# Another start offset for the stationary operands of a seven-product matrix multiply

## The chip, the cores and the metric

The kernel runs on one core of a Trainium2 chip. The metric is the device time of one execution in microseconds, taken as the median of several runs. Beside the runs there is one profiled execution, which gives the engines' busy times and a trace of every instruction and DMA.

## The reference

Linear attention without a softmax, an RMS norm with a gain, and a two-layer GELU network, all in float32:

```python
kv = np.einsum('bhsd,bhse->bhde', k, v)
out = np.einsum('bhsd,bhde->bhse', q, kv)
rms = np.sqrt(np.mean(out * out, axis=-1, keepdims=True) + 1e-06)
attn = out / rms * g_norm                      # (8, 8, 576, 64)
x = attn.transpose(0, 2, 1, 3).reshape(4608, 512)
h = x @ w_in                                   # (4608, 512) @ (512, 2048)
g = 0.5 * h * (1.0 + erf(h / sqrt(2)))
return g @ w_out                               # (4608, 2048) @ (2048, 512)
```

## The kernel before

**Chunks.** The 4,608 tokens are taken in nine chunks `c` of 512. For every chunk the kernel computes the attention output, transposed so that the 512 features lie on the partitions, the first layer `x @ w_in` with GELU, and the second layer. While chunk `c` is in its two layers, the attention of chunk `c + 1` and the key-value sums of chunk `c + 2` are done in between: small matmuls of L183 (`sum_kv`), L236 (`project_pair`) and L288 (`fold`). The order of all this is written out by hand, and every load and store goes out on SyncE's queue (SPq in the profile).

**Two halves of a number.** TensorE is fed in the float32r form. To keep float32 precision each operand is split into a high and a low part, and each product is made of three: high by high, low by high, high by low.

**Seven products.** Chunks 0 and 1 (`PLAIN = 2`) multiply in the ordinary way (L687, L714: 512 moving columns). From chunk 2 on the first layer, and from chunk 3 on (`FAST = 3`) the second layer too, cut both operands in 2 x 2 blocks and take seven products of sums of blocks instead of eight (Strassen's scheme in Winograd's form). The sums of the weights' blocks are formed once, in chunk 1 and 2, and sent to DRAM as `products`; those of `x` and `g` are formed for each chunk.

**The first layer** has 8 steps `j` of seven products. `product(at, j, k, ...)` (L545) issues one of them: two blocks of 128 rows times three parts, so six matmuls, at L552. The stationary operand is a 128 x 128 piece of a weight, the moving one 256 columns of `x`. In chunk 2 the seven products of a step come together (`layer1_pair`, L559). From chunk 3 on they are issued in two parts, products 0 to 3 (`first_part`) and 4 to 6 (`second_part`); the second part of step j stands behind the first part of step j + 1, and the small matmuls of the next chunks stand behind some of the second parts.

**The second layer** of chunks 3 to 8 has 28 ticks (`TICKS`, L464) of twelve matmuls (L1230). Here the activations are stationary and the weights are moving, 256 columns of them.

**Where the weights come from.** They do not all fit. A key, ("in", j, i) or ("out", k, n), names 512 KB: two products of the first layer or one tick of the second. Thirteen keys (`RESIDENT`) stay in SBUF. All others are loaded again for every chunk, in the order of use, into a ring of six tiles: `fetch(n)` (L498) takes tile `RING[n % 6]`, and `used` (L522) requests the key six places on when a key has been used up. So a load has some five keys' time to land.

**Where operands start.** All these tiles lie in one pool, one after the other, each a multiple of 256 bytes long, so that their starts agree modulo 256; the pieces that one matmul takes lie at multiples of 512 bytes within a tile. The tiles of the ring and of the resident keys are 64 elements, 256 bytes, longer than their 1,024 elements. `AWAY`, 48 elements or 192 bytes, says how far into such a tile the weights are put; the tiles of `x` and of the activations are always used from their start. `aligned(c, key)` (L508) names the loads that are put at 0 instead:

- of the first layer, keys with i = 0 (products 0 and 1): all eight steps in chunk 2; steps 0, 2, 3, 4 and 5 in chunks 3, 4 and 5; steps 0, 2, 3 and 4 in chunks 6 and 7; step 0 in chunk 8;
- of the second layer, the first tick, (0, 0).

From a moving operand's start to that of its stationary one it is then, modulo 256 bytes, 192 in the first layer (0 for aligned keys) and 64 in the second, where the weights are the moving side (0 in the first tick).

**How the trace shows it.** In the timeline a group x12 of L552 is two products, and a group x6 one. `h<-x,w_in` names the PSUM bank and the two operands by their tiles; since tiles are used again for other things, `w_in`, `w_out`, `x`, `s` and `r` there are names of places and no longer of contents.

Of the kernel before, what the change touches and what calls it, by code (L numbers as in the profile page):

```python
# [9 lines left out]
F32R = mybir.dt.float32r  # L10
# [13 lines left out]
FAST = 3  # L24
# [13 lines left out]
def linear_attn_rms_gelu_ffn(  # L38
# [18 lines left out]
    NT, DM = out.shape  # L57
    B, NP = kv_main.shape[:2]
# [5 lines left out]
    NCH = NT // CH  # L64
# [25 lines left out]


    LINE = 16
    AWAY = 3 * LINE
    KEPT_IN = [f"w_out{i}" for i in (4, 5, 6, 7)]
    KEPT_OUT = [f"w_out{i}" for i in (8, 9, 10, 11)] + [f"w_in{i}" for i in (13, 14, 15)]
    KEPT_OUT += ["r0", "w_in4"]
# [7 lines left out]
    def block_tile(name, dtype):  # L104
        return const.tile([P, 2 * DM + EXTRA.get(name, 0)], dtype, name=name)
# [64 lines left out]
    def rows(r):  # L170
        return slice(r * D, (r + 1) * D)
# [211 lines left out]
    def reused(i, dtype=F32):  # L383

        if i not in kept:
            kept[i] = block_tile(f"w_in{i}", dtype)
        return kept[i][:, :2 * DM]
# [10 lines left out]
    def product_out(at, src, eng=nc.sync):  # L398

        key, n = at[:-1], at[-1]  # L400
        if key in RESIDENT and key[0] == "out":
            if key not in resident:
                t = block_tile(KEPT_OUT[KEPT_KEYS.index(key[1:])], F32R)
                resident[key] = t[:, AWAY:AWAY + 2 * DM]
            to = resident[key][:, n * DM:(n + 1) * DM].rearrange("p (a n) -> p a n", a=2)
            eng.dma_start(out=to.bitcast(F32), in_=src.bitcast(F32))
            return
        if key not in products:
            products[key] = dram.tile([P, 2 * DM], F32, name="_".join(map(str, ("products", *key))))
        to = products[key][:, n * DM:(n + 1) * DM]  # L410
        eng.dma_start(out=to.rearrange("p (a n) -> p a n", a=2), in_=src.bitcast(F32))  # L411
# [3 lines left out]
    def combine(j, second):  # L415

        if not second:
            whole.clear()
            for a in range(2):
                w = parts["in", 2 * j + a].bitcast(F32)  # L420
                whole[a] = work.tile([P, DM], I32, name="z", bufs=2).bitcast(F32)
                nc.vector.tensor_tensor(out=whole[a], in0=w[:, HI], in1=w[:, LO], op=ALU.add)
                t = parts["in", 2 * j + a].rearrange("p (a n) -> p a n", a=2)
                if a == 0:
                    product_out(place_in(j, 0), t[:, :, :HALF])
                    product_out(place_in(j, 4), t[:, :, HALF:])
                else:
                    product_out(place_in(j, 3), t[:, :, HALF:])
        a11, a12 = whole[0][:, :HALF], whole[0][:, HALF:]
        a21, a22 = whole[1][:, :HALF], whole[1][:, HALF:]  # L430
        s = work.tile([P, DM], I32, name="w", bufs=2).bitcast(F32)
        s = s.rearrange("p (a n) -> p a n", a=2)
        if second:
            adds = ((s[:, 0], a11, ALU.subtract, a21), (s[:, 1], a12, ALU.subtract, whole[2]))
        else:
            whole[2] = s[:, 1]
            adds = ((s[:, 0], a21, ALU.add, a22), (s[:, 1], s[:, 0], ALU.subtract, a11))
        for o, x, op, y in adds:
            nc.vector.tensor_tensor(out=o, in0=x, in1=y, op=op)
        stage[j, second] = s  # L440
# [23 lines left out]
    TICKS = [(0, 0), (0, 1), (0, 2), (2, 0), (2, 1), (0, 3), (2, 2), (2, 3)]  # L464
# [19 lines left out]
    resident = {}  # L484
    queue = []
# [12 lines left out]
    def fetch(n):  # L498

        if n < len(queue):  # L500
            key = queue[n][1]
            i = RING[n % len(RING)]
            reused(i, F32R)
            away = 0 if aligned(*queue[n]) else AWAY
            ring[n] = kept[i][:, away:away + 2 * DM]
            nc.sync.dma_start(out=ring[n].bitcast(F32), in_=products[key])

    def aligned(c, key):  # L508

        kind, j, k = key  # L510
        if kind == "out":
            return (j, k) == TICKS[0]
        if k:
            return False
        n = 8 if c < FAST else 6 if c + 2 < B else 5 if c + 1 < NCH else 1
        return j < n and (c < FAST or j != 1)

    def operand(c, key):
        at = c, key
# [2 lines left out]
    def used(c, key):  # L522
        if (c, key) in place:
            n = place[c, key]
            ring.pop(n)
            fetch(n + len(RING))
# [5 lines left out]
        return name, block_tile(name, dtype)[:, :2 * DM]  # L532

    def keep(key):
        t = resident[key] = block_tile(KEPT_IN[key[1]], F32R)[:, AWAY:AWAY + 2 * DM]
        nc.sync.dma_start(out=t.bitcast(F32), in_=products[key])

    SETS = (("h0", "h1"), ("acc0", "acc1"), ("acc2", "acc3"))
# [266 lines left out]
    for d in range(0, 2 * D, BLK):  # L805
        h = d // D * D
        nc.gpsimd.tensor_tensor(
            out=fold[:, d:d + BLK], in0=ident[:, h:h + BLK], in1=ident[:, h + BLK:h + 2 * BLK],
# [27 lines left out]
    def sum_squares(n):  # L836
# [12 lines left out]
        out=half_g, in0=ps[:, :1], scalar1=0.5, scalar2=None, op0=ALU.mult  # L849
# [3 lines left out]
        out=sums[:, :P], lhsT=ones, rhs=eps, start=True, stop=False,  # L853
# [4 lines left out]
        out=root_g, in0=half_g, scalar1=D ** 0.5, scalar2=None, op0=ALU.mult  # L858
# [9 lines left out]
    for half in range(2):  # L868
# [6 lines left out]
        out=sums[:, :n_fold].rearrange("p (g b) -> p g b", g=2), lhsT=fold,  # L875
# [3 lines left out]
    for half in range(2):  # L879
        nc.scalar.activation(  # L880
            out=first.block((1, half)),
# [10 lines left out]
    for half in range(2):  # L892
# [3 lines left out]
            out=first.o_all[:, half], in0=first.ps.pop((0, half)), scalar=root_g, in1=bc,  # L896
            op0=ALU.mult, op1=ALU.mult,
        )
        n = 2 + half
        bc = bank(f"acc{n}")  # L900
        for t in range(NG):
            for h in range(2):
                at = column(n, t) + h
                nc.tensor.matmul(
                    out=bc[rows(h), t * P:(t + 1) * P],
# [150 lines left out]
    def later(c, i):  # L1056

        if 2 <= i < NJ2:
            raw_out(i - 2)
        if i == 7:  # L1060
            sums[c] = attn[c + 1].fold()
        if i in (5, 7):
            load_kv(c + 2, (i - 5) // 2)
        if i == 9:
            attn[c + 2].load(0)
        if i == 15:
            place_kv(c + 2, range(NP))
            attn[c + 2].load(1)
        send()
        if i == 13:  # L1070
            for n in range(2):
                fetch(n)
        if i == 15:
            for n in range(2, len(RING)):
                fetch(n)
# [39 lines left out]
    for s in range(PLAIN * NF):  # L1115
        c, i = divmod(s, NF)
# [31 lines left out]
        else:  # L1148
            spread_matmuls(c, i)
            g[s] = gelu(h.pop(s))  # L1150
            nxt, k = attn[c + 1], SQUARES.index(i) if i in SQUARES else None
# [10 lines left out]
            elif i - 1 in EARLY:  # L1162
                n = EARLY.index(i - 1)
# [209 lines left out]
    for c in range(PLAIN, FAST):  # L1373
        for j in range(NJ2):
# [28 lines left out]
            if j > 3:  # L1403
                keep(RESIDENT[j - 4])
# [92 lines left out]
```

## Time and profile before

| what | value |
|---|---|
| median of three runs | 789.97 us (789.1 to 792.87) |
| span of the profiled execution | 790.6 us |
| TensorE matmuls, busy | 779.8 us, 99% of the span, 6,460 instructions |
| TensorE weight loads, busy | 727.1 us, 92% |
| VectorE, busy | 569.6 us, 72% |
| ScalarE, busy | 351.7 us, 44% |
| DMA, mean rate over the span | 302 GB/s |

TensorE has two rows in a profile, PE for matmuls and PEld for the loads of stationary operands, which overlap the matmuls. Matmuls are pipelined: one of 256 columns is shown as some 276 ns long, but the next one starts some 113 ns after it. What one costs in a full stream is therefore the distance between starts, not the duration. The timeline merges equal instructions that follow each other: start of the first, time from there to the end of the last, and their count.

### The profile page before, as it was taken

The page shows a single profiled execution, that of the slowest core. Times are in us where ns is not written, and L with a number is a line of the kernel's source. Part 1 is how long each engine was busy: PE and PEld are TensorE (multiplying, and loading weights), DVE is VectorE, ACT ScalarE, POOL GpSimd, SP SyncE. Part 2 cuts the span into 40 slices and gives each one's busy share as a digit, 9 for nine tenths or more (in the row PEclk, how much of TensorE's full clock was granted, in tenths as well). Part 3 has the DMA queues.
Part 4 walks back from the last instruction along what each step waited for, and adds up shares of the span by engine and source line. Part 5 has one row for each costly group of instructions (what it writes and reads, how often), then busy time and mean ns, then how long its engine had stood idle before and what let it go on. Part 6 is the DMA issues. An engine that isn't in the chain of part 4 may idle for free.

```text
span 790.6 us, 16438 instructions
## 1 busy us (share of the span) xinstructions
PE 779.8 (99%) x6460; PEld 727.1 (92%) x6460; DVE 569.6 (72%) x1035; ACT 351.7 (44%) x667; POOL 162.6 (21%) x142
## 2 busy tenths in 40 slices
PE   8999999999899999999999999999999999999998
PEld 6888878888789998999999999999999999999998
DVE  3998866898467673779377956786589658965683
ACT  3777535433262232447053624363436343632461
POOL 1000040421150302350027001800161016101200
PEclk9999999999999999999999999999999999999999
DMA  9991307999999579998989799969997989799974
GB/s 347 406 390 55 121 9 272 355 349 370 344 358 320 196 278 374 364 400 293 374 333 358 259 368 333 384 231 320 322 360 252 313 307 323 248 327 343 329 252 163
DMA packets 88800, 239.10 MB, mean 302 GB/s; under 512 B 8852, under 2 KB 30612, under 8 KB 88724
## 3 DMA queue, kind: packets, MB, share of 16 engines
q1 hardware_dynamic: 88720, 238.06, 84.0%
q8 instruction: 51, 0.84, 0.4%
q14 instruction: 25, 0.20, 0.1%
q10 hardware_dynamic: 4, 0.00, 0.0%
HBM read 199.23 MB, written 34.08 MB: 295 GB/s over the span
## 4 chain that ended last, share of the span: by engine, by line
PE 94%; DMA 3%; DVE 1%; SPq 1%; issue 0%; ACT 0%; DVEq 0%; ACTq 0%
PE acc L1230 21%; PE acc L552 19%; PE acc L714 16%; PE h L552 16%; PE h L687 10%; PE a L1230 8%; PE a L236 2%; PE a L183 2%; DMA kv_main<-kv_main 1%; DMA w_in<-products_in 1%; DMA w_in<-qT 1%; PE h L677 0%; DVE x L346 0%; DVE w_out L655 0%; SPq L411 0%
## 5 line engine op out<-in xcount | busy, mean ns | idle before, releaser
L714 PE MATMUL acc<-w_out,gh 128*128 128x512 f32 x312 | 97.1, 392 | 0.0
L687 PE MATMUL h<-x,w_in 128*128 128x512 f32 x360 | 87.4, 391 | 0.6 <-DVE x L346 0.6
L687 PEld LDWEIGHTS h<-x,w_in 128*128 128x128 f32 x360 | 67.3, 188 | 15.6 <-DVE x L346 1.3
L714 PEld LDWEIGHTS acc<-w_out,gh 128*128 128x128 f32 x312 | 57.7, 188 | 12.3 <-issue 0.4
L700 ACT ACTIVATE gh<-h 128x512 fp32r<-128x512 f32 x39 | 23.3, 598 | 93.1 <-PE h L687 62.8
L714 PE MATMUL acc<-w_out,gl 128*128 128x512 f32 x156 | 60.7, 389 | 0.0
L552 PE MATMUL h<-w_in,w_in 128*128 128x256 f32 x420 | 54.8, 281 | 3.3 <-DMA w_in<-products_in 3.3
L1230 PE MATMUL acc<-w_in,w_out 128*128 128x256 f32 x444 | 55.3, 277 | 0.0
L552 PEld LDWEIGHTS h<-w_in,w_in 128*128 128x128 f32 x420 | 51.5, 192 | 3.9 <-issue 3.9
L1230 PEld LDWEIGHTS acc<-w_in,w_out 128*128 128x128 f32 x444 | 52.8, 188 | 0.0
L552 PE MATMUL acc<-w_out,w_in 128*128 128x256 f32 x390 | 52.2, 280 | 0.0
L552 PEld LDWEIGHTS acc<-w_out,w_in 128*128 128x128 f32 x390 | 47.7, 188 | 1.2 <-issue 0.9
L1230 PE MATMUL acc<-w_in,w_in 128*128 128x256 f32 x336 | 41.6, 276 | 0.0
L552 PE MATMUL acc<-w_in,w_in 128*128 128x256 f32 x300 | 41.0, 277 | 0.0
L543 DVE TENSOR_TENSOR gl<-acc,gh 128x256 f32<-128x256 f32 (+1 forms) x66 | 29.2, 443 | 15.1 <-ACT gh L589 11.0
L1230 PEld LDWEIGHTS acc<-w_in,w_in 128*128 128x128 f32 x336 | 39.8, 188 | 0.0
L278 DVE TRANSPOSE_TENSOR_REDUCE part<-sq 128x16 f32<-128x512 f32 x33 | 23.4, 709 | 20.4 <-ACT sq L268 20.4
L706 DVE TENSOR_TENSOR gl<-h,gh 128x512 fp32r<-128x512 f32 x39 | 26.8, 686 | 15.6 <-ACT h L701 15.4
L1230 PE MATMUL acc<-w_in,x 128*128 128x256 f32 x300 | 37.7, 276 | 0.0
L552 PEld LDWEIGHTS acc<-w_in,w_in 128*128 128x128 f32 x300 | 37.1, 188 | 0.5 <-issue 0.4
L589 ACT COPY gh<-h 128x256 f32<-128x256 f32 x18 | 6.7, 375 | 68.9 <-PE h L552 68.9
L552 PE MATMUL acc<-x,w_in 128*128 128x256 f32 x270 | 36.0, 278 | 0.0
(326 smaller groups left out, 1816.0 us busy)
## 6 DMA issues: line engine op xcount, KB each, us to landing
w_in<-products_in SPq DMA_DIRECT2D x172, 512.0 KB, 5.4
w_in<-products_out SPq DMA_DIRECT2D x114, 512.0 KB, 5.2
kv_main<-kv_main SPq DMA_DIRECT2D x22, 512.0 KB, 6.3
products_in<-w_in SPq DMA_DIRECT2D x40, 256.0 KB, 5.0
w_in<-w_in SPq DMA_DIRECT2D x16, 512.0 KB, 10.2
w_out<-w_out SPq DMA_DIRECT2D x16, 512.0 KB, 10.2
q<-qT SPq DMA_DIRECT2D x15, 512.0 KB, 6.7
out<-w SPq DMA_DIRECT2D x17, 256.0 KB, 4.0
```

The source lines that it names most:

```text
L183: nc.tensor.matmul(out=ps[r, n * D:(n + 1) * D], lhsT=k[:, r], rhs=v[:, r], start=(j == 0), stop=(j == NJ),)
L236: nc.tensor.matmul(out=ps[rows(h), p % 2 * HALF + a:p % 2 * HALF + e], lhsT=kv[b % 2][rows(half), p, h ^ half], rhs=q[rows(half), h, a:e], ...
L278: nc.vector.tensor_reduce(out=self.part[:, 2 * k[0] + k[1], :], in_=sq.rearrange("p (b d) -> p b d", d=BLK), op=ALU.add, axis=AX.X, apply_ ...
L543: return eng.tensor_tensor(out=out, in0=x, in1=y, op=op)
L552: nc.tensor.matmul(out=out, lhsT=y, rhs=x[:, z, kb], start=first and kb + i == 0, stop=kb == 1 and i == 2, skip_group_check=True,)
L589: nc.scalar.copy(out=u[:, left], in_=a[:, left])
L687: nc.tensor.matmul(out=h, lhsT=parts["in", i][:, w][:, p * P:(p + 1) * P], rhs=at.x[p][:, x], start=(m + p == 0), stop=(m == 2 and p == NP ...
L700: nc.scalar.activation(out=gh, in_=h, func=AF.Gelu)
L706: nc.vector.tensor_tensor(out=gl, in0=h, in1=gh.bitcast(F32), op=ALU.subtract)
L714: nc.tensor.matmul(out=ps, lhsT=x[:, ts], rhs=parts["out", i][:, w], start=(i == 0 and m == 0), stop=(m == 2 and (i == NF - 1 or (i, t) == ...
L1230: nc.tensor.matmul(out=self.bank[name][a][:, a * HALF:(a + 1) * HALF], lhsT=x[:, at], rhs=y, start=(k in (0, 2, 1) and n + p + m == 0 and ...
```

## The change

The offset of the weights becomes a matter of the layer alone: 16 elements, 64 bytes, for the first layer's keys, and 48 elements, 192 bytes, as before, for the second layer's. `aligned` goes. In every product of the first layer, and in every tick of the second, the stationary operand then starts 64 bytes (mod 256) behind the moving one. Resident keys get the same offsets. Sizes of tiles, order, loads and arithmetic stay.

```diff
     LINE = 16
-    AWAY = 3 * LINE
+    AWAY = {"in": LINE, "out": 3 * LINE}
...
-                resident[key] = t[:, AWAY:AWAY + 2 * DM]
+                resident[key] = t[:, AWAY["out"]:AWAY["out"] + 2 * DM]
...
             reused(i, F32R)
-            away = 0 if aligned(*queue[n]) else AWAY
+            away = AWAY[key[0]]
             ring[n] = kept[i][:, away:away + 2 * DM]
             nc.sync.dma_start(out=ring[n].bitcast(F32), in_=products[key])
-
-    def aligned(c, key):
-
-        kind, j, k = key
-        if kind == "out":
-            return (j, k) == TICKS[0]
-        if k:
-            return False
-        n = 8 if c < FAST else 6 if c + 2 < B else 5 if c + 1 < NCH else 1
-        return j < n and (c < FAST or j != 1)
...
     def keep(key):
-        t = resident[key] = block_tile(KEPT_IN[key[1]], F32R)[:, AWAY:AWAY + 2 * DM]
+        away = AWAY["in"]
+        t = resident[key] = block_tile(KEPT_IN[key[1]], F32R)[:, away:away + 2 * DM]
```

## The prediction

> **What bounds the kernel now.** I read the page first, then the table by stretches (one row per layer of a chunk), then the chain of waits, and then TensorE's timeline at a few places, because the change touches nothing but the addresses of operands.
>
> ```profile
> span 790.6 us, 16438 instructions
> PE 779.8 (99%) x6460; PEld 727.1 (92%) x6460; DVE 569.6 (72%) x1035; ACT 351.7 (44%) x667; POOL 162.6 (21%) x142
> PE 94%; DMA 3%; DVE 1%; SPq 1%; issue 0%; ACT 0%; DVEq 0%; ACTq 0%
> ```
> ```profile
> core 0: us, PE busy (x) PEld busy (x) DVE busy (x) ACT busy (x) POOL busy (x), PEclk, DMA share, GB/s
> 208.80:299.00 90.20, 86.90 (x647) 78.30 (x646) 57.92 (x112) 31.14 (x58) 20.34 (x20) 0.98 0.84 302
> 299.20:349.50 50.30, 50.26 (x475) 47.44 (x474) 32.07 (x63) 20.08 (x39) 22.39 (x18) 1.00 0.98 375
> 387.70:431.90 44.20, 44.20 (x469) 42.96 (x468) 30.26 (x60) 17.37 (x35) 19.49 (x14) 1.00 0.96 360
> 710.80:748.90 38.10, 38.10 (x338) 38.10 (x337) 22.43 (x42) 12.12 (x25) 7.78 (x6) 1.00 0.93 333
> ```
> TensorE carries 94% of the chain, at a granted clock of 1.00 in nearly every stretch. It does not wait; so the time is the number of matmuls times the distance from one start to the next, and a change can only win by shortening that distance. The first layer's seven products (L552) issue 7 x 8 x 6 = 336 matmuls of 256 columns in each of the chunks 2 to 8, 2,352 in all; the second layer's (L1230) issue 336 in each of the chunks 3 to 8, 2,016 in all. The last row above is the pure case: 336 matmuls, nothing between them, 38.1 us, 113.4 ns each. A second fact is in the second row: at chunk 3's first layer the DMA engines are at 0.98.
>
> **How far apart matmuls start, by address.** The code gives three distances from moving to stationary start (mod 256 bytes): 0 for the keys that `aligned` names, 192 for all other products of the first layer, 64 for the second layer (there the weights are the moving side and lie 192 on) except its first tick, at 0. The timeline merges equal instructions, so a row's start less the next row's start, over its count, is the distance.
>
> ```profile
> 710.79 1.58 PE L552 MATMUL h<-w_in,w_in 128*128 128x256 f32 x12
> 712.22 1.52 PE L552 MATMUL h<-w_out,w_in 128*128 128x256 f32 x12
> 713.58 1.52 PE L552 MATMUL acc<-w_in,w_in 128*128 128x256 f32 x12
> ```
> Chunk 8 begins with key (0, 0), at 0: (712.22 - 710.79) / 12 = 119.2 ns. The next two products lie at 192: (713.58 - 712.22) / 12 = 113.3 ns. Same line, form and clock: 5.9 ns for the address, or for the place.
>
> ```profile
> 429.66 0.98 PE L552 MATMUL acc<-w_out,w_in 128*128 128x256 f32 x6
> 430.47 0.87 PE L552 MATMUL acc<-x,w_in 128*128 128x256 f32 x6
> 431.18 0.87 PE L552 MATMUL acc<-w_in,w_out 128*128 128x256 f32 x6
> 431.88 1.60 PE L1230 MATMUL acc<-w_in,w_out 128*128 128x256 f32 x12
> 433.33 1.54 PE L1230 MATMUL acc<-w_in,w_in 128*128 128x256 f32 x12
> 434.71 1.52 PE L1230 MATMUL acc<-r,w_in 128*128 128x256 f32 x12
> 436.07 2.20 PE L1230 MATMUL acc<-w_in,w_out 128*128 128x256 f32 x18
> ```
> Here products at 192 come straight after small matmuls of another form (L183), and they do not run at 113.3: (431.88 - 430.47) / 12 = 117.5 ns, to the end of the layer. Then the tick at 0: (433.33 - 431.88) / 12 = 120.8. Then 64: 115.0 in the first twelve, (436.07 - 434.71) / 12 = 113.3 in the next, and so it stays:
>
> ```profile
> 313.60 5.02 PE acc L552 x42
> 349.68 21.86 PE acc L1230 x192
> 421.61 4.76 PE acc L552 x42
> 640.36 5.02 PE acc L552 x42
> 672.78 21.86 PE acc L1230 x192
> ```
> These rows are of the chain. 192 matmuls of the second layer take 21.86 us, 113.9 ns, in chunk 3 and in chunk 7 alike, settling included. So 192 has two paces, a quick one after a product at 0 and a slow one after a switch of form, and keeps either. At 64 only the quick one is seen, and a stream that comes from 120.8 reaches it within twelve matmuls.
>
> ```profile
> 307.48 1.58 PE L552 MATMUL acc<-w_out,w_in 128*128 128x256 f32 x12
> 308.89 1.58 PE L552 MATMUL acc<-x,w_in 128*128 128x256 f32 x12
> 310.30 0.87 PE L552 MATMUL h<-w_in,w_in 128*128 128x256 f32 x6
> ```
> ```profile
> 339.98 0.84 PE L552 MATMUL acc<-w_out,w_out 128*128 128x256 f32 x6
> 340.86 1.65 PE L552 MATMUL acc<-w_out,w_in 128*128 128x256 f32 x12
> 342.35 1.57 PE L552 MATMUL acc<-x,w_in 128*128 128x256 f32 x12
> 343.76 0.87 PE L552 MATMUL h<-w_in,w_in 128*128 128x256 f32 x6
> ```
> Chunk 3 has two long stretches at 117.5 ns: after the second layer of chunk 2 (L714), and from 340.86 on. The second starts behind a short wait: the six matmuls before it take 0.88 us instead of 0.68, in the stretch where the DMA share is 0.98. I take that for a ring load that is just late.
>
> **The sum, part by part.**
>
> 1. Keys at 0 go to 64. By `aligned` these are, two products each, 8 parts of chunk 2, 5 of chunks 3, 4 and 5, 4 of chunks 6 and 7, 1 of chunk 8: 8 + 15 + 8 + 1 = 32 parts, 64 products, 384 matmuls. At 5.9 ns: 2.3 us.
>
> 2. The second layer's first tick goes from 0 to 64, twelve matmuls in six chunks, with the settling behind it: 72 x (120.8 - 113.3) + 72 x (115.0 - 113.3) = 0.66 us.
>
> 3. Products at 192 go to 64. Those in the quick pace gain nothing (113.3 both). Those in the slow one gain 117.5 - 113.3 = 4.2 ns: 42 matmuls from 307.48, 42 from 340.86, 18 each at the ends of chunks 3, 4 (the rows from 429.66) and 5, and some 18 behind the wait in chunk 2: about 156, 0.65 us.
>
> 4. What 64 itself costs after a switch of form is in no row, since today a product at 0 or 192 always stands there. From below it costs nothing; from above it never leaves 117.5 (a rival, below). The nearest row is the one at 433.33: 1.7 ns x 12 = 0.02 us to settle. There are some 30 such places (8 pairs of chunk 2, 5 to 6 in chunks 3 to 5, 3 in chunks 6 and 7): 30 x 0.02 = 0.6 us given back.
>
> 5. Places where a shorter distance only lengthens a wait:
>
> ```profile
> 208.81 1.59 PE L552 MATMUL h<-x,w_in 128*128 128x256 f32 x12
> 210.28 1.65 PE L552 MATMUL h<-w_in,w_in 128*128 128x256 f32 x12
> 215.24 0.48 PE L552 MATMUL h<-w_in,w_in 128*128 128x256 f32 x2 [3.30 <-DMA w_in<-products_in]
> ```
> Chunk 2's first 24 matmuls run up against a load that ends at 215.2 whatever TensorE did: their share, 24 x some 5 ns = 0.12 us, is lost. Likewise chunk 3 up to 340.86: 60 matmuls at 0 and 42 at the longer distance stand ahead of the late load, 60 x 5.9 + 42 x 4.2 = 0.53 us. A ring tile released earlier is requested earlier, but at a DMA share of 0.98 the request only queues longer. I count all of it lost. In chunks 4 to 8 the loads go at 0.93 to 0.96 and no wait is on the chain; 0.3 us in 44 is well inside that.
>
> 6. DMAs, their number, bytes and queue are the same; tiles keep their size (64 spare elements), so nothing else moves. VectorE and ScalarE follow TensorE in these layers and are busy 30.26 and 17.37 us of 44.20: they do not become the bound.
>
> Sum: 2.3 + 0.66 + 0.65 - 0.6 - 0.12 - 0.53 = 2.4 us. The profiled execution would go from 790.6 to 788.2; it stands 0.6 us above the median of the three runs, 789.97, so the median would go to 787.6, 0.3% down. The three runs lie 3.8 us apart, and about 0.5%, 3.95 us, is what a measurement of this kernel can tell from no change. I expect a real gain too small to be called one.
>
> **Rivals.**
>
> *Everything settles and nothing is lost (0.12).* If 64 takes the quick pace at once after a switch, and chunk 3's loads move up with the releases, only the 0.12 us of chunk 2 is lost: 3.5 us, a median of 786.5; some more if a switch itself gets cheaper. For it: the settling after 433.33 starts from a worse pace than a fresh stream may have. Against: the DMA share of 0.98.
>
> *The place sets the pace, not the address (0.16).* All products at 0 stand first after something: a switch of form, or a change of layer. If the first dozen matmuls there are slow at any address, only part 3 and some of part 2 can be saved, under 1 us, and with chunk 3's loss nothing is left: 790. For it:
>
> ```profile
> 645.57 0.83 PE L236 MATMUL a<-q,kv 64*64 64x256 f32 x12
> 646.33 1.69 PE L552 MATMUL h<-w_in,w_in 128*128 128x256 f32 x12
> 647.85 0.84 PE L552 MATMUL h<-s,w_in 128*128 128x256 f32 x6
> ```
> After L236 the first twelve take 1.52 us, and much of that is the switch. Against it: at 710.79 there is no switch of form before the slow dozen, and the pace drops to 113.3 exactly where the key at 0 ends. The Trainium skill speaks for this rival: its page "SBUF — State Buffer", section "Who interferes with whom", gives TensorE two independent read ports, one for the moving operand and one for the weight load, and says that it never waits on anyone. By that rule no offset could matter and the time would stay at 790. The trace does not agree where two paces, 119.2 and 113.3, stand in one line with equal forms.
>
> *64 also has a slow pace after a switch, and now nothing resets it (0.12), slower.* At 192 the slow pace lasts until a product at 0 comes. The change removes every one of these. If the stream at 64 takes 117.5 after L236 or L183, it keeps it through the second layer as well, which lies at 64 too, to the next switch, which starts it again: 12 x 336 = 4,032 matmuls of chunks 3 to 8 x 4.2 ns = 16.9 us, less the 3.6 of parts 1 to 3: some 13 us more, 803. It decides from 3.6 us / 4.2 ns = 860 slow matmuls on, the first layers of two and a half chunks. For it: exactly that happens at 192. Against: six second layers came to 64 from a slow stream, in chunks 3 to 5 from 117.5 by way of 120.8, and all settled.
>
> **How the numbers follow.** Forecast 0.60, the rivals 0.12, 0.16 and 0.12. The likeliest time is 787.6. Without the slow rival the cases lie between 786.5 and 790; with about 1.3 us on each side for the scatter of the runs the range is 785.2 to 791.3, and what it leaves out is mainly the 0.12. Faster by over 0.5% (below 786.0) needs the first rival or a lucky forecast: 0.2. Slower by over 0.5% is the last rival and a little scatter: 0.14. Within 0.5%: 0.66.
>
> **What would show it.** In the profile after, the first twelve matmuls of chunk 8's first layer should take 1.36 us instead of 1.43, and the row of 42 at the end of chunk 4's first layer should show 113.3 instead of 117.5. The second layer's 192 matmuls should take 21.76 us instead of 21.86. Chunk 3's wait near 340 should grow by up to 0.5 us, and the one at 215 should end when it does now. Rows at 117.5 after L236 or L183 that go on into the second layer would prove the slow rival; rows at 119 to 121 at the places of today, the rival of place. I am wrong in the sum, not in the mechanism, if all paces are 113.3 and the span is still at 790: then the loads took it.

## The result, and the profile after

The change makes the kernel slower: 802.73 us, the median of six runs (799.61 to 803.75), against 791.33 for the kernel before in six runs (789.1 to 794.19). The ratio is 1.0138, 95% interval 1.0117 to 1.0159. The likeliest time of the prediction, 787.6, lies on the other side, and its range does not reach the result. The last rival had 803.

The page of the changed kernel, its first lines and the chain by engine (its own lines stand nine lower: L543 is L552 of before, L1221 is L1230, L705 is L714):

```profile
span 801.0 us, 16438 instructions
PE 789.5 (99%) x6460; PEld 736.9 (92%) x6460; DVE 569.1 (71%) x1035; ACT 351.5 (44%) x667; POOL 162.5 (20%) x142
PE 91%; DMA 4%; DVE 3%; SPq 1%; issue 0%; ACT 0%; DVEq 0%; ACTq 0%
```

The same instructions, the same bound, and 10.4 us more of it: TensorE is busy 9.7 us longer. Two views say where. First the table by stretches, of before and then of after, for the second layer of chunk 3 and the first layers of chunks 4 and 8, of after also for the first layer of chunk 3:

```profile
349.52:387.70 38.18, 38.18 (x338) 38.18 (x337) 29.24 (x49) 18.66 (x36) 0.00 (x0) 1.00 0.92 334
387.70:431.88 44.18, 44.18 (x468) 42.94 (x467) 30.26 (x60) 17.35 (x35) 19.49 (x14) 1.00 0.96 360
710.79:748.93 38.14, 38.14 (x338) 38.14 (x337) 22.46 (x42) 12.12 (x25) 7.78 (x6) 1.00 0.93 333
```
```profile
301.02:350.82 49.80, 49.80 (x475) 47.17 (x474) 32.04 (x63) 19.61 (x39) 22.32 (x18) 1.00 1.00 377
350.82:390.40 39.58, 39.58 (x338) 39.58 (x337) 29.23 (x49) 19.06 (x36) 0.00 (x0) 1.00 0.89 326
390.40:434.72 44.32, 44.32 (x468) 43.07 (x467) 30.19 (x60) 17.34 (x35) 19.45 (x14) 1.00 0.97 356
719.86:759.43 39.57, 39.57 (x338) 39.57 (x337) 22.72 (x42) 12.28 (x26) 7.76 (x6) 1.00 0.91 324
```

The second layer of chunk 3 has the same 336 matmuls, no wait and a clock of 1.00 in both, and 1.40 us more. Those of chunks 4 to 7 have 1.40 more as well: 5 x 1.40 = 7.0 us. Chunk 8's first layer has 1.43 more. The rest is small: chunk 2 takes 91.82 us for 90.41, chunk 3's first layer 49.80 for 50.30, chunks 4 to 7 together 0.8 more in theirs, and chunk 2 begins 0.4 later.

Then the chain of waits of the changed kernel, which has the first 192 matmuls of each second layer as one row:

```profile
350.99 22.61 PE acc L1221 x192
434.89 22.61 PE acc L1221 x192
...
759.60 21.78 PE acc L1221 x192
```

The rows left out are those of chunks 5 to 7, alike. 22.61 / 192 = 117.8 ns in chunks 3 to 7, 21.78 / 192 = 113.4 ns in chunk 8; before, all six stood at 21.86. But the addresses of these matmuls have not changed, except for the first twelve. So it is not the address of a matmul that sets its pace: the same instructions at the same addresses run at either. The timeline shows where it turns over. Chunk 4, then the end of chunk 7 and of chunk 8's first layer:

```profile
433.36 0.84 PE L543 MATMUL acc<-x,w_in 128*128 128x256 f32 x6
434.04 0.84 PE L543 MATMUL acc<-w_in,w_out 128*128 128x256 f32 x6
434.72 1.58 PE L1221 MATMUL acc<-w_in,w_out 128*128 128x256 f32 x12
436.14 1.58 PE L1221 MATMUL acc<-w_in,w_in 128*128 128x256 f32 x12
```
```profile
719.86 1.58 PE L543 MATMUL h<-w_in,w_in 128*128 128x256 f32 x12
721.27 1.58 PE L543 MATMUL h<-w_out,w_in 128*128 128x256 f32 x12
```
```profile
759.43 1.54 PE L1221 MATMUL acc<-w_in,w_in 128*128 128x256 f32 x12
760.81 1.52 PE L1221 MATMUL acc<-w_in,w_out 128*128 128x256 f32 x12
```

In chunk 4 the first layer ends at (434.72 - 433.36) / 12 = 113.3 ns, and the second begins at (436.14 - 434.72) / 12 = 118.3. The long pace then goes on into the next first layer until small matmuls come between. Chunk 8 has none: its whole first layer runs at (721.27 - 719.86) / 12 = 117.5, and there the change of layer turns the pace the other way, to 115.0 in the first tick and 113.4 over the 192.

Below, the pace of a stream is its distance from start to start, "quick" is 113.3 ns and "long" 117.8; a stretch of twelve, read from starts that are printed to 0.01 us, is good to some 0.8 ns, so 117.5 and 118.3 are both the long pace. "Distance" alone is from the moving to the stationary start, modulo 256 bytes unless 128 is named. A "zero" is a product or tick whose weights are put at 0, and "the change of layer" is that from the first layer to the second.

### The profile page after: what moved, and what is told of

It reads as the page before. It is cut to its first block, busy times and chain, and to the rows that moved or that the text cites. A ratio compares the mean times of both kernels' runs of the same rounds, so it can differ in the third digit from the quotient of the medians.

```text
span 801.0 us, 16438 instructions
## 1 busy us (share of the span) xinstructions
PE 789.5 (99%) x6460; PEld 736.9 (92%) x6460; DVE 569.1 (71%) x1035; ACT 351.5 (44%) x667; POOL 162.5 (20%) x142
## 4 chain that ended last, share of the span: by engine, by line
PE 91%; DMA 4%; DVE 3%; SPq 1%; issue 0%; ACT 0%; DVEq 0%; ACTq 0%
PE acc L1221 21%; PE acc L543 18%; PE h L543 16%; PE acc L705 14%; PE a L1221 8%; PE h L678 8%; PE a L236 2%; PE a L183 2%; DMA kv_main<-kv_main 1%; DMA w_in<-products_in 1%; DMA out<-z 1%; DMA w_in<-qT 1%; DMA q<-qT 1%; SPq L411 1%; PE h L668 0%
## 5 line engine op out<-in xcount | busy, mean ns | idle before, releaser
L705 PE MATMUL acc<-w_out,gh 128*128 128x512 f32 x312 | 97.2, 393 | 0.0
L705 PEld LDWEIGHTS acc<-w_out,gh 128*128 128x128 f32 x312 | 57.7, 188 | 12.3 <-ACT h L692 0.3
L705 PE MATMUL acc<-w_out,gl 128*128 128x512 f32 x156 | 60.9, 390 | 0.0
L543 PE MATMUL h<-w_in,w_in 128*128 128x256 f32 x420 | 56.3, 286 | 4.1 <-DMA w_in<-products_in 4.1
L543 PEld LDWEIGHTS h<-w_in,w_in 128*128 128x128 f32 x420 | 53.1, 194 | 4.6 <-issue 4.6
L1221 PE MATMUL acc<-w_in,w_out 128*128 128x256 f32 x444 | 56.6, 280 | 0.0
L1221 PEld LDWEIGHTS acc<-w_in,w_out 128*128 128x128 f32 x444 | 53.9, 189 | 0.0
L543 PE MATMUL acc<-w_out,w_in 128*128 128x256 f32 x390 | 52.4, 280 | 0.0
L543 PEld LDWEIGHTS acc<-w_out,w_in 128*128 128x128 f32 x390 | 48.0, 188 | 1.0 <-issue 0.7
L1221 PE MATMUL acc<-w_in,w_in 128*128 128x256 f32 x336 | 42.8, 280 | 0.0
L543 PE MATMUL acc<-w_in,w_in 128*128 128x256 f32 x300 | 41.5, 279 | 0.0
L1221 PEld LDWEIGHTS acc<-w_in,w_in 128*128 128x128 f32 x336 | 40.8, 189 | 0.0
L1221 PE MATMUL acc<-w_in,x 128*128 128x256 f32 x300 | 38.9, 281 | 0.0
L543 PEld LDWEIGHTS acc<-w_in,w_in 128*128 128x128 f32 x300 | 37.6, 188 | 0.5 <-issue 0.4
L1221 PEld LDWEIGHTS acc<-w_in,x 128*128 128x128 f32 x300 | 36.8, 189 | 0.0
```

What stands on the lines that cost most here:

```text
L543: nc.tensor.matmul(out=out, lhsT=y, rhs=x[:, z, kb], start=first and kb + i == 0, stop=kb == 1 and i == 2, skip_group_check=True,)
L705: nc.tensor.matmul(out=ps, lhsT=x[:, ts], rhs=parts["out", i][:, w], start=(i == 0 and m == 0), stop=(m == 2 and (i == NF - 1 or (i, t) == ...
L1221: nc.tensor.matmul(out=self.bank[name][a][:, a * HALF:(a + 1) * HALF], lhsT=x[:, at], rhs=y, start=(k in (0, 2, 1) and n + p + m == 0 and ...
```

## The experiments

Every kernel has all of the computation. Times stand against the kernel before, run beside them; where one profile is enough the trace decides.

### One half put back: the first tick at 0

```diff
-            away = AWAY[key[0]]
+            away = 0 if key == ("out", *TICKS[0]) else AWAY[key[0]]
```

> The changed kernel with one thing put back: the weights of the second layer's first tick lie at 0 again, in each of the chunks 3 to 8 (72 matmuls). Carried pace (a stream keeps its pace until something resets it, and the tick at 0 was the reset): the second layers of chunks 3 to 7 fall from 39.6 to 38.2 us, 5 x 1.4 = 7.0 us; chunk 8's first layer no longer takes over 117.8 ns, 1.4 us; the first parts of chunks 4 to 7 likewise, some 1.1 us; the tick itself costs 0.6. Together 801 - 9 = 792 us. Address (64 in the first layer is the worse place, or the tick's own address is all that counts): 72 matmuls at 120 instead of 118, 801 us, and the second layers stay at 117.8 ns.

Measured: 794.95 us against 792.2, ratio 1.0034 (1.0013 to 1.0054), span 792.4. The first of six equal rows of the chain, then chunk 8's first layer in the table by stretches:

```profile
349.04 21.86 PE acc L1221 x192
```
```profile
711.15:750.73 39.58, 39.58 (x339) 39.58 (x338) 22.73 (x42) 12.31 (x26) 7.75 (x6) 1.00 0.90 322
```

Twelve matmuls at 0 ahead of each second layer give back all 7 us. The rest of the expectation failed: chunk 8's first layer follows a quick second layer and is as long as ever. That the span came out at 792 is an accident: chunk 2 begins 0.6 us earlier and waits less for its load (2.99 us for 4.08).

### The other half put back: the first layer's keys at 0

```diff
-            away = AWAY[key[0]]
+            away = 0 if aligned(*queue[n]) else AWAY[key[0]]
...
+    def aligned(c, key):
+        kind, j, k = key
+        if kind == "out" or k:
+            return False
...
```

> The changed kernel with the other half put back: the first layer's 64 products of before lie at 0 again, the second layer's first tick stays at 64 from its moving side. Carried pace: the first layers are as quick as in the kernel before (chunk 2 back by 0.6 us, chunk 8 by 1.4), but all six second layers are entered from a quick first layer with no reset and run at 117.8 ns, 6 x 1.4 us: about 798 us. Address: products at 64 are what costs, and only a sixth of them is taken away: 800 us, second layers unchanged.

Measured: 799.35 us against 792.2, ratio 1.0085 (1.0056 to 1.0114). The first of six rows of the chain that agree to 0.01 us:

```profile
350.89 21.78 PE acc L1229 x192
```

The time is the expected one and the reason is not: all six second layers are quick, and the first layers are long (39.58 us in chunk 8).

### Both halves put back: only 64 for 192

```diff
-    AWAY = 3 * LINE
+    AWAY = {"in": LINE, "out": 3 * LINE}
```

(with `away = 0 if aligned(*queue[n]) else AWAY[key[0]]`)

> The kernel before with its zeros kept everywhere and only 192 replaced by 64 in the first layer. Carried pace: both resets are there, so 64 and 192 differ only in the stretches where 192 ran at 117.5 ns: 790 us, between 0.7 us faster than before and equal; second layers at 113.6 ns. Address: 64 in the first layer is slower than 192 by itself, 795 us or more.

Measured: 799.86 us against 792.2, ratio 1.0094 (1.0064 to 1.0124). My first theory, that a product at 0 resets a stream to the quick pace, falls here. Chunk 8's first layer in the timeline:

```profile
716.81 1.58 PE L553 MATMUL h<-w_in,w_in 128*128 128x256 f32 x12
718.23 1.58 PE L553 MATMUL h<-w_out,w_in 128*128 128x256 f32 x12
719.64 1.58 PE L553 MATMUL acc<-w_in,w_in 128*128 128x256 f32 x12
```

After the dozen at 0 (118.3 ns) the products at 64 run at (719.64 - 718.23) / 12 = 117.5, where those at 192 ran at 113.3 in the same place. Which pace follows a product at 0 depends on the step that follows it, to 64 or to 192. Nor is it that 64 is worse in itself: second layers, where the distance is 64 as well, are quick in this very run.

### No zeros, 192 throughout

```diff
-    AWAY = {"in": LINE, "out": 3 * LINE}
+    AWAY = {"in": 3 * LINE, "out": 3 * LINE}
```

> The kernel before with no product at 0: 192 in the whole first layer, second layer as in the changed kernel. Carried pace: what is lost is the reset, not the offset: first layers at 117.5 ns after every switch of form, second layers at whichever pace the change of layer leaves, so between 795 and 803 us. Address: 192 keeps its 113.3 ns and the 64 products at 0 gain 5.9 ns each: 788 to 790 us.

Measured: 798.12 us against 792.2, ratio 1.0068 (1.0049 to 1.0087). Second layers, by the chain:

```profile
514.17 21.77 PE acc L1221 x192
593.41 22.61 PE acc L1221 x192
```

Chunks 3 to 5 are quick, 6 and 7 long, 8 quick. In the timeline the first layers of chunks 3, 4, 5 and 8 end long, those of 6 and 7 quick. So the change of layer turned the pace over six times out of six, and taking the zeros away costs at 192 too. From a second layer into a first one at 192 the pace goes on as it is (quick into chunks 4 to 6, long into 7 and 8).

### What the distance itself costs

All weights at 0, then at 128, then both layers 32 and 96 behind (mod 128), always without zeros:

```diff
-    AWAY = {"in": LINE, "out": 3 * LINE}
+    AWAY = {"in": 0, "out": 0}
```
```diff
-    AWAY = {"in": LINE, "out": 3 * LINE}
+    AWAY = {"in": 2 * LINE, "out": 2 * LINE}
```
```diff
-    AWAY = {"in": LINE, "out": 3 * LINE}
+    AWAY = {"in": LINE // 2, "out": 7 * LINE // 2}
```
```diff
-    AWAY = {"in": LINE, "out": 3 * LINE}
+    AWAY = {"in": 3 * LINE // 2, "out": 5 * LINE // 2}
```

> No offset anywhere: stationary and moving operands of both layers start alike (mod 256) in all 4,368 matmuls of 256 columns. Both theories: 120 ns at every one. The kernel before has 3.6 us over 113.3 ns in these matmuls, this one 4,368 x 6.7 ns = 29.3 us: 816 us.

> 128 bytes in both layers, no zeros. Two phases (64 and 192 are alike modulo 128 and each knows the paces 113.3 and 117.8; 0 and 128 are alike too): 120 ns everywhere, 816 us. Distance (operands disturb each other when they start in the same 64 of 256 bytes, and 128 is the farthest from that): 113.3 ns everywhere whatever came before, 787 us.

> No zeros, and both layers' stationary operands 32 bytes behind the moving ones (mod 128: weights at 32 in the first layer, at 224 in the second). Two phases of 64-byte pieces: where two operands share a piece for part of the time every matmul pays part of the price, so one pace between 113.3 and 120 ns in all layers, 800 to 810 us. Only whole 64 bytes count: as at 0, 120 ns, 816 us. If 32 were clear of both, 113.3 ns everywhere, 787 us.

> No zeros, stationary operands 96 bytes behind the moving ones (mod 128: weights at 96 in the first layer, at 160 in the second). Two phases of 64-byte pieces: the same pace as at 32, or its mirror image, 800 to 810 us. Only whole 64 bytes count: as at 64, with its two paces, some 800 us. If 96 were clear of both, 113.3 ns everywhere, 787 us.

Measured, one run each: 816.85, 815.29, 810.44 and 809.08 us. One row of the chain of each, in this order; with 96 the later chunks have a second pace:

```profile
351.69 23.04 PE acc L1221 x192
```
```profile
354.95 22.78 PE acc L1221 x192
```
```profile
436.56 22.72 PE acc L1221 x192
```
```profile
436.60 22.79 PE acc L1221 x192
603.64 22.53 PE acc L1221 x192
```

Over 192: 120.0 ns at 0, 118.6 at 128, 118.3 at 32, 118.7 or 117.3 at 96. So 128 bytes, the farthest that two starts can be apart in 256, is nearly as dear as 0: to within 1.4 ns the distance counts modulo 128, not 256. Only at 64 modulo 128, which is 64 and 192 alike, was the quick pace seen, and there it is one of two.

### Does the change of layer turn the pace over?

From the kernel before, its zero at the first tick alone is taken away:

```diff
         if kind == "out":
-            return (j, k) == TICKS[0]
+            return False
```

> The kernel before with one zero taken away, that of the second layer's first tick. Flip (the change of layer alone turns a stream's pace over, as in the runs so far: quick in, slow out; slow in, quick out): chunks 3 to 5, whose first layers end at 117.5 ns, get quick second layers of 38.1 us, a little shorter than today; chunks 6 to 8, whose first layers end at 113.3, get second layers at 117.8 ns, 39.6 us. 790.6 + 3 x 1.4 - 3 x 0.1 = 794.5 us. Carried pace (the pace goes over the change of layer unchanged): chunks 3 to 5 slow, 6 to 8 quick, likewise 794.5 us in total but in the other chunks. Reset needed nowhere: 790.1 us.

Measured: 796.22 us against 792.55, ratio 1.0061 (1.004 to 1.0081), span 793.9.

```profile
349.04 21.77 PE acc L1230 x192
...
513.58 21.77 PE acc L1230 x192
592.71 22.61 PE acc L1230 x192
...
751.01 22.61 PE acc L1230 x192
```

Chunks 3 to 5, whose first layers end long, are quick, and 6 to 8, whose first layers end quick, are long, chunk by chunk as a turn at the change of layer has it, and against the pace being carried over.

### The step after a zero, in the second layer

The kernel before, zeros and all, with the second layer's weights at 64:

```diff
-    AWAY = 3 * LINE
+    AWAY = {"in": 3 * LINE, "out": LINE}
```

> The kernel before, zeros included, with the second layer's weights at 64 instead of 192, so that its stationary operands lie 192 behind the moving ones instead of 64. Two phases: which of the paces follows a product at 0 depends on which operand moves on and by how much; in the first layer a jump to 192 gave the quick and one to 64 the slow pace, so a jump to 64 gives six second layers at 117.8 ns, 790.6 + 6 x 1.4 = 799 us. Offset alone (192 is the good distance in the first layer, so it is in the second): 790 us, second layers of 38.2 us as before.

Measured: 799.82 us against 792.55, ratio 1.0099 (1.0067 to 1.0131). All six rows of the chain are as this one:

```profile
348.81 22.64 PE acc L1231 x192
```

After a tick at 0, weights stepping to 192 give the quick pace (before, and the first experiment) and to 64 the long one. In the second layer 64 for the weights means a distance of 192, so the distance that is quick after a zero in the first layer is long after a zero in the second. It is the step of the weights, -64 or +64 modulo 256, whichever side of the matmul they are on. The pace ahead of the zero does not matter: in the kernel before, chunks 3 to 5 come to it long and 6 to 8 quick, and all six leave it quick. As every zero lies at 0, the step and the address that it leads to cannot be told apart here.

### Where exactly it turns

From the run without the zero at the first tick: in chunk 6 the first tick's activations are put 64 bytes into their tile and its weights at 0; in chunk 7 the zero stands at the second tick.

```diff
...
-            return False
+            return (c, j, k) in ((6, *TICKS[0]), (7, *TICKS[1]))
...
-            op = self.ops[i] = take(F32R)
+            if (self.c, i) == (6, 0):
+                name = free.pop(0)
...
+                op = self.ops[i] = name, block_tile(name, F32R, LINE)
+            else:
+                op = self.ops[i] = take(F32R)
```

(`block_tile` takes the place in the tile as a third argument, and the tile of these activations is made 256 bytes longer.)

> The run without any zero at the first tick, with two small edits. Chunk 6: the first tick's activations start at 64 in their tile and its weights at 0, so that they stay 64 apart, but the one weight load that meets a moving operand with the same start (mod 128) falls from the change of layer (where the first stationary piece, at 0, is loaded beside the last moving one, at 0) to the change from tick 0 to tick 1. Chunk 7: the zero stands at the second tick instead of the first. Meeting (that one load turns the pace over): chunk 6 has its tick 0 at 113.3 ns as the first layer before it, and 117.8 from tick 1 on; chunk 7 has tick 0 at 117.8, tick 1 near 120 and 113.3 from tick 2 or 3 on; chunk 8 as before 117.8 throughout. Change of layer (another line, bank and operands turn the pace over): chunk 6 at 117.8 from tick 0 on. Chunks 3 to 5 at 113.3 by both. Time some 792.5 us.

Measured: 796.66 us, one run. The timeline at the change of layer, chunk 6 and chunk 7:

```profile
594.93 1.52 PE L1236 MATMUL acc<-w_in,s 128*128 128x256 f32 x12
596.29 1.58 PE L1236 MATMUL acc<-w_in,x 128*128 128x256 f32 x12
597.71 1.58 PE L1236 MATMUL acc<-r,x 128*128 128x256 f32 x12
```
```profile
675.45 1.58 PE L1236 MATMUL acc<-w_in,w_out 128*128 128x256 f32 x12
676.87 1.59 PE L1236 MATMUL acc<-w_in,x 128*128 128x256 f32 x12
678.30 1.54 PE L1236 MATMUL acc<-r,w_out 128*128 128x256 f32 x12
679.68 1.52 PE L1236 MATMUL acc<-w_in,s 128*128 128x256 f32 x12
```

In chunk 6 the first tick keeps the 113.3 ns of the layer before it ((596.29 - 594.93) / 12), and the second has 118.3. The turn has moved by one tick with the addresses; the change of line, bank and operands, which stayed where it was, does not turn the pace by itself. What it moved with is one of three things that the edit shifted together: the weight load whose start meets that of the moving operand beside it (the expectation), the moving operand's step from 0 to 192, and the stationary operand's step to 0. This is one place in one run, and it does not tell them apart. That a meeting is not enough shows elsewhere: from a second layer into a first one at 192 without a zero, both operands at the turn start at 192, and in all ten such places (five in the run with 192 throughout, five in the last experiment) the pace goes on unchanged. In chunk 7 the tick ahead of the zero is long (118.3), the zero costs 119.2, and after one tick of settling it is quick. The span, 794.9 us, is 2.4 above the time expected. Against the run without the zero at the first tick, chunk 2 takes 1.1 us longer (its wait is treated below), the first layer of chunk 3 0.6, and chunk 2 begins 0.65 later.

### A version by the rules found

The kernel before without the zeros that the flip makes needless: the first tick's in chunks 3 to 5, the first key's in chunks 4 to 8.

```diff
-            return (j, k) == TICKS[0]
+            return (j, k) == TICKS[0] and c + 2 >= B
...
-        return j < n and (c < FAST or j != 1)
+        return j < n and (c < FAST or j != 1 and (j or c == FAST))
```

> The kernel before without the zeros that the runs so far say are not needed: the second layer's first tick in chunks 3 to 5 (their first layers end at 117.5 ns, and the change of layer turns that into the quick pace) and the first key of chunks 4 to 8 (the quick pace of a second layer goes on into a first layer at 192). The other zeros stay. Flip: second layers of 38.1 us in chunks 3 to 5 and 38.2 in 6 to 8, first layers shorter by some 0.06 us each, 0.6 us together: 0.1%, not to be told from no change by the times, but by the trace. If the flip holds only by chance of these runs: second layers at 39.6 us in some chunks, 792 us or more.

Measured: 791.95 us against 792.18, ratio 1.0003 (0.9983 to 1.0022): no difference that can be told. From the second layer of chunk 3 on the stretches are as expected, here the first layers of chunks 4 and 8:

```profile
387.60:431.72 44.12, 44.12 (x468) 42.88 (x467) 30.27 (x60) 17.33 (x35) 19.50 (x14) 1.00 0.97 364
710.27:748.36 38.09, 38.09 (x339) 38.09 (x337) 22.46 (x42) 12.12 (x25) 7.77 (x6) 1.00 0.94 339
```

44.12 for 44.18 and 38.09 for 38.14; the second layers take 38.10, 38.09 and 38.10 us in chunks 3 to 5, 38.18 in 6 and 7. The rules foretell these stages to a twentieth of a microsecond, and what they save in all of them together is 0.5 us. Chunk 2 and the first layer of chunk 3, where loads are waited for, moved by 0.3 and 0.2 us in opposite directions, which the rules do not foretell.

## Why the prediction was wrong

**The step that failed** is the reading "at 64 only the quick one is seen", ahead of the sum. It was true of the trace and proved nothing: all six streams at 64 had come by way of a tick at 0 and a step of the weights to 192, so the six were one observation. Without that tick, five of the six second layers ran at 117.8 ns at the same distance of 64, 1.40 us more each, where the prediction had 113.3 in all. The rows from chunk 4 that I quoted held both halves of the matter, a pace that is kept and a zero that ends it, and I applied it to 192 and not to 64. The argument against the last rival, that six second layers had settled, was the same six.

**Part 2, the first tick.** I counted the zero as a cost, 0.66 us to be saved. Taking it away costs 5 x 1.40 = 7.0 us, and putting back only this returns them.

**Part 1, the keys at 0.** 2.3 us were to be saved at 5.9 ns a matmul. The dozens at 0 did get shorter, from 119.2 to 117.5 at the start of chunk 8, and everything behind them longer: chunk 8's first layer lost 1.43 us, chunks 4 to 7 0.8 together. In chunk 2 every first-layer stretch behind ordinary second-layer matmuls (L714 of before) is now long from its start, the first one here:

```profile
209.20 1.58 PE L543 MATMUL h<-x,w_in 128*128 128x256 f32 x12
210.62 1.58 PE L543 MATMUL h<-w_in,w_in 128*128 128x256 f32 x12
216.27 0.98 PE L543 MATMUL h<-w_in,w_in 128*128 128x256 f32 x3 [4.08 <-DMA w_in<-products_in]
```

(210.62 - 209.20) / 12 = 118.3 from the first matmul on, though at 64.

**Part 3, the stretches at 117.5.** Half right: the ends of the first layers of chunks 3 to 5 did become quick, as at 433.36 above, and so did chunk 3's stretch from 340.86 on. The stretch after chunk 2's second layer stayed long. The sign that was to show this named the wrong row: the 42 matmuls near the end of chunk 4's first layer were quick before the change (4.76 us from 421.61 on, 113.3 ns each), and only the last 18 were long.

**Part 4, the cost of 64 after a switch.** The bound from above, that it never leaves 117.5, was the right one after ordinary second-layer matmuls (L714), and the value that I took, 0.02 us to settle, holds in some places and not in others: in chunk 3 of the changed kernel, products after L236 are quick once and long the next time, here from the second dozen behind each.

```profile
316.87 1.52 PE L543 MATMUL acc<-x,w_in 128*128 128x256 f32 x12
318.23 0.84 PE L543 MATMUL acc<-w_in,w_in 128*128 128x256 f32 x6
```
```profile
322.90 1.58 PE L543 MATMUL h<-x,w_in 128*128 128x256 f32 x12
324.32 0.87 PE L543 MATMUL acc<-w_in,w_in 128*128 128x256 f32 x6
```

(318.23 - 316.87) / 12 = 113.3, (324.32 - 322.90) / 12 = 118.3.

**Part 5, the waits.** The load in chunk 2 did not end when it did before: 216.27 for 215.24, with a later start of the chunk. Chunk 3's late load is gone, its first layer is 0.5 us shorter; that it now begins 1.8 us later, with more time for the loads, is the likely reason and was not tried.

**The rivals.** The last one had the time, 803 for 802.73, its sign and its principle, that nothing resets the stream any more. Its place was wrong: it had the long pace begin after L236 and L183 and be carried into the second layer. First layers of chunks 3 to 7 end quick, and it is the change of layer that makes the stream long. That the sums meet is chance: it counted twelve long layers, 16.9 us, and took 3.6 us of savings off; the trace has five second layers and one first layer long, 8.4 us, and chunk 2 and some stretches besides. The rival of place was half right: pace does depend on what stands before. The Trainium skill's rule behind it, in "SBUF — State Buffer", section "Who interferes with whom", that TensorE's two read ports are independent and that it never waits on anyone, would leave no offset that matters, and these runs do not agree: all operands at 0 cost 816.85 us against 792.55, and nothing but start addresses differs.

**What stays open.** Why the step decides which pace follows a zero; which of the three things shifted together turns the pace at the change of layer; why a first layer at 64 is long after a second layer of either pace, while one at 192 takes the pace over, though both meet an equal start (mod 128) there; and what decides after L236 and L183, where both paces were seen at one and the same offset (behind L288 without a zero, only the quick one was). The traces show the order of events and not what TensorE's reads wait for.

## What to carry to other kernels

When the same instruction with the same addresses shows two durations in one trace, look at what came before it, and count independent histories, not rows: what always stands behind a reset has shown nothing about itself without one. A step that looks like pure cost in its own rows (here 12 matmuls at 120 ns) may be what keeps the next 324 at 113.3. Before such a step is removed everywhere, remove it in one place and read the stage behind it.

## What the runs showed of the hardware that was not expected

For float32r matmuls of 256 columns, one weight load each, the distance from start to start is 113.3 ns or 117.8 when stationary and moving operand start 64 bytes apart modulo 128, and 118.6 to 120.0 at 0 and 128. Between the two paces the stream has a memory. It survived 336 matmuls without a break. Between the first layer and the second, with no zero there, it turned over in all 32 places of these runs where the weights lay at 64 or 192 and the activations at their tile's start, both ways; in the one place where the two were shifted, it turned a tick later.

A second thing moves the times of this kernel from run to run. In the 52 runs of the kernel before that stand beside the experiments, the span was 786.8 to 789.8 us in the 11 with a mean granted clock of 1.000 and 791.3 to 793.4 in the 13 with 0.995. One place where the clock drops is in chunk 2: TensorE waits for a load there, and afterwards the granted clock can be lower for a while. In the kernel before the wait is 3.30 us; in the run with 192 throughout, by the table of waits:

```profile
PE h L543 <- DMA w_in<-products_in: 2.8, 1, 2.8
```

The stretch from 205 to 225 us in the table by stretches, of the kernel before, of that run, of the run that tells where the pace turns, and of the changed kernel (the granted clock is the third number from the end):

```profile
205.00:225.00 20.00, 16.70 (x144) 14.90 (x141) 8.46 (x17) 6.67 (x14) 3.47 (x4) 0.91 0.97 356
```
```profile
205.00:225.00 20.00, 17.21 (x163) 15.71 (x158) 9.29 (x19) 7.45 (x15) 5.33 (x6) 1.00 1.00 376
```
```profile
205.00:225.00 20.00, 16.44 (x137) 14.59 (x132) 8.12 (x16) 5.77 (x12) 2.55 (x2) 0.83 1.00 367
```
```profile
205.00:225.00 20.00, 15.92 (x149) 14.41 (x144) 7.96 (x16) 5.69 (x12) 2.25 (x2) 0.91 0.99 356
```

After a wait of 3.30 us the clock is 0.91 over this stretch, after 2.79 it stays at 1.00, after 3.56 in the third kernel it is 0.83, and after 4.08 in the changed one 0.91 again. The run without the zero at the first tick also waited 3.56 us and had 0.91, so the length of the wait does not decide alone. Chunk 2 in the third kernel takes 91.6 us, for 90.4 in the kernel before. The gap belongs to the load of the first products and was left alone.
